# Hedgehog attention and Sinkhorn-routed experts on one core: q projections on row halves, one exponential for a pair's scalings, the routing table in PSUM, and a new step order

## The chip, the core and the metric

One core of a Trainium2 chip runs the whole program in one launch. TensorE (PE in the profile, PEld for its weight loads), VectorE (DVE), ScalarE (ACT) and GpSimd (POOL) each work through a queue of their own, in the order in which the kernel was written out; SyncE (SP), POOL and ACT issue DMAs. The metric is the device time of one execution in microseconds, the median of several.

## The reference, cut to what matters

```python
def phi(x):                                   # x: q or k, [8 batches, 8 heads, 576, 64]
    proj = np.einsum('bhsd,df->bhsf', x, w_phi)             # 128 features
    proj = proj - np.max(np.abs(proj), axis=-1, keepdims=True)
    return np.concatenate([np.exp(proj), np.exp(-proj)], axis=-1)
kv = np.einsum('bhsf,bhsd->bhfd', k_p, v);  z = np.sum(k_p, axis=2)
x = np.einsum('bhsf,bhfd->bhsd', q_p, kv) / den             # den from q_p and z
# x as [4608, 512]; then 8 experts, all of them for every row
P = np.exp(x @ w_gate - max)                                # [4608, 8]
for _ in range(8):
    P /= P.sum(1, keepdims=True) + 1e-09
    P /= P.sum(0, keepdims=True) + 1e-09;  P *= N / E
for e in range(8):
    out += P[:, e:e + 1] * (np.maximum(x @ w1[e], 0.0) @ w2[e])
```

## The kernel before, in words

A planner (`Plan`) holds every instruction as an operation with an engine, a duration and the buffers that it reads and writes. It lists them out engine by engine: the one that can start first by its own model goes next, and among equals the one that was written first. `Links` is its model of two DMA lines (SP's and POOL's), `LINK` the table of rates, `Clock` its model of TensorE's clock. What comes out is a fixed order for each engine; on the chip an engine waits at the head of its queue for whatever is late.

**Attention.** 32 pairs of heads (8 batches of 4) go through steps that a string, `order`, names letter by letter: `l`, `e` load q, k, v; `t` turns q and k by a DMA transpose (batches 2 to 7; batches 0 and 1 are turned on TensorE); `a` projects k, takes the maxima of its absolute values (`maxes`, L614) and writes exp of plus and minus the projection (`exp`, L618); `q` projects q with tokens on partitions for its maxima; `p` projects q again with features on partitions for its exponentials; `b` multiplies keys and values; `n` and `m` form the numerators of the two heads (L905, L913, L918, L919); `c` turns the result into `xT`; `r` does the 64 remaining tokens of a batch; `g` the gate. `u` and `d` are expert 0 (first and second product, 24 and 20 steps), put between the others so that TensorE has work. A q or k projection of a pair holds two heads in 128 rows of contraction, 64 rows each, and `wphi2` is block-diagonal: half of each such product is by zeros.

The maxima lie in a small tile `m`. For a pair ACT takes two small exponentials: `em` of plus and minus k's maxima, which scales v (POOL, L810, then L816 for the column of ones), and `r` of minus twice q's maxima, which scales the first half of the numerators on DVE (L913). The rest step has the same two, `em_r` and `r_r`.

**Routing.** When attention's buffers are given up (`swap`), eight rounds run on DVE (L1161 to L1188): scale the table's columns, sum its rows, reciprocal, scale the rows, sum the columns, split the sums into three bf16 parts, add them over partitions by a product with ones (TensorE, `colw`), reciprocal. The tables lie in SBUF. TensorE meanwhile goes on with expert 0 (`up0`, `down0`), and the routing's eight products stand in its queue between these. P is ready after L1189.

**Experts 1 to 7.** Each product is done by a Strassen-like scheme (L1481, L1472, L1613); sums of quarters of x and of the weights are taken by `sub` (L1240) on DVE first. For expert 1 these sums also wait for P. `UNITS` holds orders of the steps, the first nine for expert 1.

PSUM has 8 banks; `PP`, `P1`, `PO` are rings of single banks.

Of the kernel before, what the change touches and what calls it, by code (L numbers as in the profile page):

```python
# [126 lines left out]
class Links:  # L127
# [13 lines left out]
    def step(self, t, work):  # L141
# [5 lines left out]
        if len(on) == 2:  # L147
            a, b = (x[0][2] for x in self.line)
            all_ = (0.61 if a.turn else 0.84) / (a.unit + b.unit)
            share = [all_ * a.unit, all_ * b.unit]  # L150
# [48 lines left out]
class Plan:  # L199
# [10 lines left out]
    def op(self, eng, dur, lat, fn, r=(), w=(), takes=(), nbytes=0, shared=False):  # L210
# [5 lines left out]
        o.shared, o.turn, o.unit, o.tiled = shared, False, 0, 0  # L216
# [54 lines left out]
    def schedule(self):  # L271
# [22 lines left out]
        while len(done) < len(self.ops) or links.next():  # L294
# [10 lines left out]
            if landed and (best is None or landed[0] <= best[0]):  # L305
                o = links.land(*landed)
                o.end = landed[0] + 1.0
                finish(o)
                continue
# [40 lines left out]
def kernel(  # L350
# [38 lines left out]
    colw = const.tile([128, 128], BF16, name="colw")  # L389
# [13 lines left out]
    wphi2f = wphi2.rearrange("p a b -> p (a b)")  # L403

# [17 lines left out]
    def pool(el, fn, r=(), w=()):  # L422
        plan.op("POOL", el * 1.68e-3 + 0.13, 0.15, fn, r, w, shared=True)

    LINK = {320: (325, 56), 150: (160, 40), 230: (470, 108), 250: (305, 50), 280: (380, 60),
            270: (500, 48), 90: (340, 75), 148: (265, 30), 160: (540, 50)}

    def dma(queue, nbytes, rate, fn, r=(), w=()):

        speed, unit = LINK.get(rate, (rate, 40))  # L430
        if nbytes == 2 << 20:
            speed, unit = 400, 150
        o = plan.op(queue, 0.8 if queue == "POOL" else 0.6, 0.0, fn, r, w, (), nbytes / speed)
        o.turn, o.unit = rate == 148, unit

    TI, GR, KM, QM, PM, NM, RM = 0, 0, 0, 0, 0, 0, 0
# [36 lines left out]
    ring(a_s, [128, NP], FP32, "r_r", 2)  # L473
    ring(a_s, [128, 3, 8], FP32, "m", 2, 1)
    ring(a_s, [128, 2, 8], FP32, "em", 2, 1)
    ring(a_s, [128, 2, NP], FP32, "em_r", 2)
    ring(a_t, [128, 2, 8, D1], BF16, "v", 2, 1)
    ring(a_s, [128, 2, 5], FP32, "r", 2, 1)
    ring(a_s, [128, 1, 5], FP32, "rec", 3, 1)
# [16 lines left out]
    ring("s_p", [128, NT], FP32, "rr", 1)  # L496
    ring("s_p", [128, 3, E], FP32, "cs", 1)
    ring("s_p", [128, E], FP32, "c_bc", 1)
# [125 lines left out]
    def two(merged):  # L624

        if merged:
            b = new("P2")
            return [b], [lambda: b()[:, 0:512], lambda: b()[:, 512:1024]]
        b = [new("PP") for _ in range(2)]
        return b, b  # L630

    def tokens(pp, stat, n, r, takes=()):

        if not TI:
            for c in range(n):
                pe(256, lambda c=c: mm(pp[1][2 * c // n]()[:, 1024 // n * c % 512:][:, 0:256],
                                       stat(c), wphi2f, True, True),
                   r + ["wphi2"], [pp[0][2 * c // n * (len(pp[0]) - 1)]], takes)
            return

        def rows():
            for c in range(n):
                for x in range(2):
                    nc.tensor.matmul(pp[1][x]()[:, 128 * c:128 * c + 128],
                                     lhsT=stat(c)[64 * x:64 * x + 64],
                                     rhs=wphi[64 * x:64 * x + 64], start=True, stop=True)

        o = plan.op("PE", n * 0.056, 0.22, rows, r + ["wphi"], pp[0], takes)
        o.tiled = 1

    def feature_rows(pt, mov, r):

        if not TI and not GR:
            for x in range(2):
                pe(512, lambda x=x: mm(pt[1][x]()[:, 0:512], wphi2[:, x, :], mov(), True, True),
                   r + ["wphi2"], [pt[0][x * (len(pt[0]) - 1)]])
            return

        def rows():
            for x in range(2):  # L660
                half = slice(64 * x, 64 * x + 64)
                nc.tensor.matmul(pt[1][x]()[:, 0:512], lhsT=wphi[half], rhs=mov()[half],
                                 start=True, stop=True)

        o = plan.op("PE", 0.222, 0.22, rows, r + ["wphi"], pt[0])
        o.tiled = 1

    def rest_a(b, t):
# [23 lines left out]
        r["r"] = new("r_r")  # L692
        r["em"] = new("em_r")
        own = r["E"] + r["T"] + [m, r["r"], r["em"]]
        pp = two(RM)
        tokens(pp, lambda c: rT()[:, c, :], NP, [rT], own)
        if TI:
            mk = [(m, x) for x in range(2)]
            for x in range(2):
                maxes(512, lambda x=x: m()[:, 2 * x], lambda x=x: pp[1][x]().rearrange(  # L700
                    "p (c f) -> p c f", c=NP), [pp[0][x * (1 - RM)]], [(m, x)])
            for x, s in ((0, 1.0), (1, -1.0)):
                exp(512, lambda x=x: r["E"][x]().rearrange("p a b -> p (a b)"),
                    lambda: pp[1][1](), s, pp[0][-1:], [(r["E"][x], 0)])
        else:
            mk = [(m, c) for c in range(2 - RM)]
            for c in range(2 - RM):
                n = NP // 2 * (1 + RM)

                def sc(c=c, n=n):  # L710
                    return pp[0][c]().rearrange("p (a b c) -> p a b c", a=n, b=2)

                maxes(256 * n, lambda c=c, n=n: m()[:, 0:3:2, n * c:n * c + n].rearrange(
                    "p b a -> p a b"), sc, [pp[0][c]], [(m, c)])
                for x, s in ((0, 1.0), (1, -1.0)):
                    exp(128 * n, lambda x=x, c=c, n=n: r["E"][x]()[:, n * c:n * c + n],
                        lambda sc=sc: sc()[:, :, 1, :], s, [pp[0][c]], [(r["E"][x], c)])
        r["Ek"] = [[(r["E"][x], c) for c in range(1 if TI else 2 - RM)] for x in range(2)]
# [7 lines left out]
        exp(10, lambda: r["r"](), lambda: m()[:, 0], -2.0, mk, [r["r"]])  # L726
        pool(8, lambda: nc.gpsimd.tensor_scalar_mul(m()[:, 1], m()[:, 2], -1.0), mk, [(m, "neg")])
        em, vd = r["em"], vrd[b % 2]
        exp(10, lambda: em(), lambda: m()[:, 1:3], 1.0, mk + [(m, "neg")], [em])
        for h in range(2):  # L730
# [4 lines left out]
                in1=em()[rows, :, :, None].to_broadcast([64, 2, NP, D]), op=ALU.mult),  # L735
                [(t["v"], h), em], [("vrd", b % 2, h)])
            pool(80, lambda rows=rows, h=h: nc.gpsimd.tensor_copy(
                out=vd[rows, :, :, h, D], in_=em()[rows]),
# [3 lines left out]
    def pair_a(b, pr, t):  # L742

        h0 = (2 * pr) % 4
        s = {}
        if b < 2:
# [26 lines left out]
        s["r"] = new("r")  # L773
        em = new("em")
        own = s["E"] + s["T"] + [s["v"], em, m, s["r"]]
        at = (0, 2)

        def scores(x, pp):

            merged = (QM, KM)[x]  # L780
            for i, buf in enumerate(pp[0]):
                n = 1 + merged
                if TI or (GR and x == 0):
                    def src(buf=buf, n=n):
                        return buf().rearrange("p (h c f) -> p h c f", h=n, c=4)

                    def part(full, i=i, n=n):
                        return full.rearrange("p (c h) f -> p h c f" if len(full.shape) == 3
                                              else "p (c h) -> p h c", h=2)[:, i:i + n]
                else:  # L790
                    def src(buf=buf, n=n):
# [1273 lines left out]
```

## Time and profile before

| | |
|---|---|
| time, median of 3 runs | 1009.07 us (1008.1 to 1009.47) |
| span of the profiled execution | 1007.1 us, some 2.0 us below the median |
| attention, by the last copy into `xT` | from 0 to about 203.8 us |
| routing, L1164's first start to L1189's end | 205.1 to 242.1 us |
| first product of expert 1 (L1481) | 244.2 us |
| busy: PE, DVE, ACT, POOL | 99%, 89%, 81%, 44% |

A matmul's record runs from its issue to its modelled end; the next one starts while it drains. What a matmul takes from TensorE is thus the distance between starts in a row of them, not its duration. The same holds for back-to-back instructions on ACT and DVE, whose records overlap.

### The profile page before, as it was taken

The numbers are of one execution on the slowest core, as the hardware profiler recorded it, in microseconds if no ns is written. First come the engines' busy times: TensorE is split into PE (matmuls) and PEld (weight loads), VectorE is DVE, ScalarE is ACT, GpSimd is POOL, SyncE is SP. The second block draws the span as 40 slices with busy tenths as digits, with TensorE's granted clock in tenths as the row PEclk, the third lists the DMA queues.
The fourth block names the chain that finished last, engine by engine and source line by source line (L and its number), as shares of the span: only waits on it lengthen the run. The fifth ranks groups of instructions, "written<-read, shape, count | busy, mean of one in ns | idle before, by whom it ended". The sixth has DMA issues, their size and how long they took to land.

```text
span 1007.1 us, 23304 instructions
## 1 busy us (share of the span) xinstructions
PE 993.4 (99%) x8376; PEld 728.2 (72%) x8376; DVE 897.1 (89%) x1999; ACT 813.2 (81%) x1930; POOL 447.0 (44%) x514
## 2 busy tenths in 40 slices
PE   7899999999999999999999999999999999999998
PEld 5666666644566877777777877787778777787775
DVE  7999998987898898899989898989889988989886
ACT  7999999835979788878878788778887888778884
POOL 5778674400133344434444444444443444344443
PEclk9999999999999999999999999999999999999999
DMA  9999999181136423282327133632246222724653
GB/s 253 190 194 171 166 152 145 38 170 56 53 119 148 145 97 98 84 186 96 112 97 166 46 100 127 135 127 99 97 119 176 97 98 84 148 79 143 206 177 126
DMA packets 129748, 128.86 MB, mean 128 GB/s; under 512 B 55776, under 2 KB 98272, under 8 KB 129632
## 3 DMA queue, kind: packets, MB, share of 16 engines
q1 hardware_dynamic: 97680, 103.33, 35.5%
q0 software_dynamic: 31648, 23.86, 17.4%
q8 instruction: 65, 1.06, 0.4%
q14 instruction: 51, 0.42, 0.1%
q10 hardware_dynamic: 304, 0.20, 0.1%
HBM read 122.50 MB, written 19.53 MB: 141 GB/s over the span
## 4 chain that ended last, share of the span: by engine, by line
PE 92%; ACT 3%; DVE 2%; DMA 2%; issue 1%; POOL 0%; SPq 0%; DVEq 0%
PE ps L1472 42%; PE ps L1481 21%; PE ps L622 15%; PE ps L1613 11%; PE ps L905 2%; DMA xp<-xT 1%; ACT k L618 1%; ACT q L618 1%; DMA xi<-X 1%; PE ps L752 0%; DVE m L614 0%; ACT wx L618 0%; DVE wx L614 0%; DMA acc<-in_k_dram 0%; PE ps L934 0%
## 5 line engine op out<-in xcount | busy, mean ns | idle before, releaser
L1881 POOL TENSOR_TENSOR acc<-acc,hx 128x512 f32<-128x512 f32 x186 | 235.1, 1271 | 403.4 <-ACT hx L1878 138.5
L1472 PEld LDWEIGHTS <-hs 128*128 128x128 bf16 x1984 | 194.1, 98 | 46.6 <-issue 0.2
L1878 ACT ACTIVATE hx<-ps,P 128x256 f32<-128x256 f32 x372 | 159.3, 484 | 53.3 <-PE ps L1472 51.9
L1866 DVE SCALAR_TENSOR_TENSOR acc<-ps,P,acc 128x256 f32<-128x256 f32 x372 | 162.0, 477 | 29.8 <-PE ps L1472 28.1
L1481 PE MATMUL ps<-xT,T 128*128 128x512 bf16 x608 | 170.7, 379 | 0.0
L1472 PEld LDWEIGHTS <-hx 128*128 128x128 bf16 x1488 | 145.6, 98 | 25.1
L1472 PE MATMUL ps<-hx,hs 128*128 128x256 bf16 x992 | 144.3, 273 | 0.0
L1682 DVE CUSTOM_DVE_ANT_0 hs<-ps,U 128x512 bf16<-128x512 f32 x192 | 124.7, 684 | 10.9 <-PE ps L1481 6.6
L1613 PE MATMUL ps<-xT 128*128 128x256 bf16 x576 | 125.4, 272 | 0.0
L1481 PEld LDWEIGHTS <-T 128*128 128x128 bf16 x672 | 65.7, 98 | 40.4
L1688 ACT ACTIVATE hs<-ps 128x512 bf16<-128x512 f32 x96 | 55.8, 598 | 41.1 <-PE ps L1481 39.7
L1472 PE MATMUL ps<-wx,hs 128*128 128x256 bf16 x560 | 78.5, 273 | 0.0
L622 PE MATMUL ps<-w,hx 128*128 128x512 bf16 x288 | 73.0, 379 | 0.0
L622 PE MATMUL ps<-xT,w 128*128 128x512 bf16 x288 | 72.9, 379 | 0.0
L1472 PE MATMUL ps<-wx,hx 128*128 128x256 bf16 x496 | 72.6, 273 | 0.0
L1682 DVE CUSTOM_DVE_ANT_0 hs<-ps,X 128x512 bf16<-128x512 f32 x96 | 65.1, 683 | 7.4 <-PE ps L1613 6.6
L1472 PE MATMUL ps<-hx 128*128 128x256 bf16 x496 | 71.2, 273 | 0.0
L1613 PEld LDWEIGHTS <-xT 128*128 128x128 bf16 x576 | 56.3, 98 | 17.4
L614 DVE TENSOR_REDUCE m<-ps 128x4 f32<-128x512 f32 x88 | 58.8, 680 | 4.2 <-PE ps L622 2.0
L1472 PE MATMUL ps<-w,hx 128*128 128x256 bf16 x432 | 62.2, 273 | 0.0
L1678 ACT COPY X<-ps 128x512 f32<-128x512 f32 x96 | 58.6, 611 | 2.5 <-DVE ps L1656 2.4
L1472 PE MATMUL ps<-w,hs 128*128 128x256 bf16 x432 | 60.2, 273 | 0.0
(174 smaller groups left out, 2256.4 us busy)
## 6 DMA issues: line engine op xcount, KB each, us to landing
xT<-xi SPq DMA_DIRECT2D x48, 448.0 KB, 4.3
xT<-xd SPq DMA_DIRECT2D x72, 256.0 KB, 3.9
wx<-in_moe_w_dram POOLq DMA_DIRECT2D x8, 1024.0 KB, 11.0
v_m<-in_v_dram SPq DMA_DIRECT2D x15, 512.0 KB, 5.0
out_dram<-acc SPq DMA_DIRECT2D x14, 512.0 KB, 2.9
w<-in_moe_w_dram POOLq DMA_DIRECT2D x6, 1024.0 KB, 11.0
xT<-xp SPq DMA_DIRECT2D x24, 256.0 KB, 2.7
qk<-in_k_dram POOLq DMA_DIRECT2D x12, 256.0 KB, 5.2
```

Source lines behind the costliest of these rows:

```text
L614: dve(el, lambda: nc.vector.tensor_reduce(out=dst(), in_=src(), axis=AX.X, op=ALU.max, apply_absolute_value=True), r, w)
L618: act(el, lambda: nc.scalar.activation(out=dst(), in_=src(), func=ACT.Exp, bias=0.0, scale=scale), r, w)
L622: nc.tensor.matmul(out_, lhsT=lhsT, rhs=rhs, start=start, stop=stop)
L1472: pe(256, lambda i=i, k=k, z=z: nc.tensor.matmul(bank()[:, 256 * i:256 * i + 256], lhsT=lhs(k, i), rhs=rhs(k), start=first and z, stop=k = ...
L1481: pe(512, lambda k=k: nc.tensor.matmul(bank().rearrange("p (a b) -> p a b", a=2), lhsT=lhs(k), rhs=rhs(k), start=first and k == 0, stop=k ...
L1613: pe(256, lambda: nc.tensor.matmul(halves_of(bank[q], n)(), lhsT=lhs(), rhs=t()[:, rhs, :], start=start, stop=True, skip_group_check=True) ...
L1678: act(512, lambda: nc.scalar.copy(out=flat(to[q])(), in_=bank[q]()), [bank[q]], [(to[q], 0), (to[q], 1)])
L1682: dve(515, lambda: nc.vector._custom_dve(ADD_SAT, out=out_(q, i, j), in0=bank[q]().rearrange("p (a b) -> p a b", a=2), in1=to[q](), s0=3.0 ...
L1688: act(512, lambda: nc.scalar.activation(out=out_(q, i, j), in_=bank[q]().rearrange("p (a b) -> p a b", a=2), func=ACT.Relu, bias=0.0, scal ...
L1866: dve(320, lambda n=n, ts=ts: nc.vector.scalar_tensor_tensor(out=acc[g][:, ts, 256 * j:256 * j + 256], in0=bank()[:, 256 * n:256 * n + 256 ...
L1878: act(370, lambda n=n: nc.scalar.activation(out=u()[:, n, :], in_=bank()[:, 256 * n:256 * n + 256], func=ACT.Copy, bias=0.0, scale=P[:, 4 ...
L1881: pool(695, lambda: nc.gpsimd.tensor_tensor(out=acc[g][:, 2 * i:2 * i + 2, 256 * j:256 * j + 256], in0=acc[g][:, 2 * i:2 * i + 2, 256 * j: ...
```

## The change

Six parts. (1) **q on row halves**, for pairs 8 to 31: steps `q` and `p` become one block of ten matmuls that contract over 64 rows each, one head's rows against `wphi` (the plain weights, twice, one copy on each half of the partitions), alternately on the upper and lower half; it takes four PSUM banks at once. (2) **One exponential a pair**: POOL multiplies the maxima of k and q by -1 and -2 (`signs`), and one ACT instruction writes all 24 values into `em`; the scaling of v moves from step `a` to behind step `q`. The rest step likewise. (3) **Routing in PSUM**: one bank holds the table, the row sums and the column sums; POOL writes a transposed copy of L, so that both sums run over neighbouring words; the ones product is fp32 and replaces the split into three parts. (4) For expert 1 the sums of w1 and of the first pair of x run on POOL instead of DVE, and those of w1 no longer wait for P. (5) `down0` of groups 5 and 6 is read by ACT alone. (6) The planner's DMA constants, `order` and the first nine entries of `UNITS` are new. (A switch `JOINT` for joined numerators is added; its sets are empty.)

```diff
@@ class Links
-        self.line[n].append([at + (3.1 if n else 1.6), o.nbytes / 1e3, o])
+        lag = (2.4 if n else 2.1) if o.turn else 3.1 if n else 1.6
...
-    LINK = {320: (325, 56), 150: (160, 40), 230: (470, 108), 250: (305, 50), 280: (380, 60),
...
+    LINK = {320: (352, 245), 150: (355, 28), 230: (447, 41), 250: (305, 50), 280: (404, 58),
...
+    ROWS = range(8, 32)
+    JOINT = {"k": (), "q": (), "p": (), "n": ()}
@@ pair_a: behind k's exponentials
-        pool(8, lambda: nc.gpsimd.tensor_scalar_mul(m()[:, 1], m()[:, 2], -1.0), mk, [(m, "neg")])
-        exp(16, lambda: em(), lambda: m()[:, 1:3], 1.0, mk + [(m, "neg")], [em])
-        pool(1024, lambda: nc.gpsimd.tensor_tensor(
-            out=s["v"]()[:, :, :, 0:D],
...
@@ pair_a, maxima()
-            if GR:
-                pts[0] = two(PM)
+            if halves_:
+                pts[0] = two(pm)
+                more = [z for y in pts[0] for z in y]
 
                 def rows():
                     for c in range(4):
                         for x in range(2):
                             half = slice(64 * x, 64 * x + 64)
-                            nc.tensor.matmul(pq[1][x]()[:, 128 * c:128 * c + 128],
+                            nc.tensor.matmul(banks_[x]()[:, 128 * c:128 * c + 128],
                                              lhsT=qkT(0, c, 1)[half], rhs=wphi[half],
                                              start=True, stop=True)
                     for x in range(2):
                         half = slice(64 * x, 64 * x + 64)
-                        nc.tensor.matmul(pts[0][1][x]()[:, 0:512], lhsT=wphi[half],
+                        nc.tensor.matmul(more[x]()[:, 0:512], lhsT=wphi[half],
                                          rhs=qkT(0, 0, 4)[half], start=True, stop=True)
...
-            exp(10, lambda: s["r"]()[:, :, 0:4],
-                lambda: m()[:, 0].rearrange("p (a b) -> p a b", a=2), -2.0,
-                mq, [(s["r"], 0)])
+            pool(16, lambda: nc.gpsimd.tensor_tensor(
+                out=m()[:, 1:3], in0=m()[:, 0:3:2],
+                in1=signs[:, 0:2, None].to_broadcast([128, 2, 8]), op=ALU.mult),
+                mk + mq + ["signs"], [(m, "neg")])
+            exp(24, lambda: em()[:, 0:24], lambda: m().rearrange("p a b -> p (a b)"), 1.0,
+                mk + mq + [(m, "neg")], [(em, 0)])
+            pool(1024, lambda: nc.gpsimd.tensor_tensor(
+                out=s["v"]()[:, :, :, 0:D],
...
@@ down0
-            if ts % 2:
+            if ts % 2 or g in (5, 6):
@@ routing, one round
+            if it:
+                dve(366, lambda: nc.vector.tensor_tensor(
+                    out=table(), in0=L, in1=c()[:, None, :].to_broadcast([128, NT, E]),
+                    op=ALU.mult), lk, [bank])
+            dve(366, lambda src=table if it else lambda: L: nc.vector.tensor_reduce(
+                out=rr(), in_=src(), axis=AX.X, op=ALU.add), lk, [bank])
+            dve(291, lambda: nc.vector.reciprocal(out=rr(), in_=rr()), [], [bank])
+            dve(366, lambda: nc.vector.tensor_tensor(
+                out=turned(), in0=Lt(), in1=rr()[:, None, :].to_broadcast([128, E, NT]),
+                op=ALU.mult), [(side, 0)], [bank])
+            dve(366, lambda: nc.vector.tensor_reduce(
+                out=cs()[:, 0], in_=turned(), axis=AX.X, op=ALU.add), [bank], [cs])
+            pe(240, lambda: mm(sums(), ones(), cs()[:, 0], True, True), [cs, (side, 1)], [bank])
...
@@ sums_up
-        late = ["late"] + (["P"] if e == 1 else [])
+        late, eng = ["late"], pool if e == 1 else dve
```

How the orders move, at three places. First TensorE in attention: where steps `q` and `p` of a pair stand side by side before the change (`wphi_90` is `wphi2`, `qkT` the turned q):

```order
L622 LDWEIGHTS qkT
L622 MATMUL ps<-wphi_90,qkT 128x256
L622 LDWEIGHTS wphi_90
L622 MATMUL ps<-qkT,wphi_90 128x512
L622 LDWEIGHTS wphi_90
L622 MATMUL ps<-qkT,wphi_90 128x512
L905 LDWEIGHTS q_2093
L905 MATMUL ps<-kv,q_2093 128x65
```

These are the last of four 256-column products, then the two 512-column ones and the next step. And the end of such a block after the change, with the expert-0 product behind it:

```order
L804 LDWEIGHTS qkT
L804 MATMUL ps<-wphi,qkT 128x128
L809 LDWEIGHTS wphi
L809 MATMUL ps<-qkT,wphi 128x512
L809 LDWEIGHTS wphi
L809 MATMUL ps<-qkT,wphi 128x512
L623 LDWEIGHTS hx
L623 MATMUL ps<-w_1061,hx 128x512
```

Six products (four of 256 columns, two of 512) became ten (eight of 128, two of 512), in one piece. Second, DVE in the routing, one round before and one round after (L1161 and L1194 scale the columns, L1167 and L1200 the rows):

```order
L1185 TENSOR_REDUCE c_bc<-ps 128x8
L1188 RECIPROCAL c_bc<-c_bc 128x8
L1161 TENSOR_TENSOR T<-L,c_bc 128x288
L1164 TENSOR_REDUCE rr<-T 128x36
L1166 RECIPROCAL rr<-rr 128x36
L1167 TENSOR_TENSOR T<-L,rr 128x288
L1170 TENSOR_REDUCE cs<-T 128x8
L1179 TENSOR_TENSOR cs<-cs 128x8 x2
```

```order
L1194 TENSOR_TENSOR ps<-L,ps 128x288
L1197 TENSOR_REDUCE ps<-ps 128x36
L1199 RECIPROCAL ps<-ps 128x36
L1200 TENSOR_TENSOR ps<-T,ps 128x288
L1203 TENSOR_REDUCE cs<-ps 128x8
L1207 RECIPROCAL ps<-ps 128x8
```

Nine instructions a round became six. In TensorE's queue the eight routing products now stand exactly 14 expert-0 products of 512 columns apart, where before it was 18 to 24; 20 such products lie between the gate's last product and the first routing product, and 13 between the last routing product and the first product of expert 1. Third, POOL behind attention's last scaling of v (`X` holds sums of x, `T` and `wx` sums of w1):

```order
L824 TENSOR_TENSOR v<-v_m,em 128x16x64
L831 CAST v<-em 128x16
L518 DMA wx<-in_moe_w_dram 128x4x1024
L518 DMA wx<-in_moe_w_dram 128x8x512
L1261 TENSOR_TENSOR X<-xT 128x1024
L1189 COPY T<-L 128x288
L1261 TENSOR_TENSOR xT<-xT 128x2x2x256
L1261 TENSOR_TENSOR X<-xT 128x1024
L1261 TENSOR_TENSOR X<-xT 128x256
L1261 TENSOR_TENSOR X<-xT,X 128x1024
L1261 TENSOR_TENSOR T<-wx 128x1024
```

Before, the two weight loads were followed there by expert 1's additions to `acc`; the sums stood in DVE's queue. SP's queue is the same in its first 25 DMAs.

More of the change, by code (lines that the diff above doesn't have):

```diff
@@ L651, in feature_rows @@
[L651 to L666, printed above, removed]
+        return [b] if merged else [b[:1], b[1:]]
@@ L668, in rest_a, with feature_rows @@
+    def feature_rows(pp, mov, r):
+        for x in range(2):
+            pe(512, lambda x=x: mm(pp[x]()[:, 0:512], wphi2[:, x, :], mov(), True, True),
+               r + ["wphi2"], [pp[x]])
     def rest_a(b, t):
```

401 lines of the change are left out of this document (203 added, 198 removed), and 50 rows, old and new, of the table UNITS.

## The prediction

> **What bounds the kernel now.** First the page: span, busy time by engine, and the chain of work that ended last.
>
> ```profile
> span 1007.1 us, 23304 instructions
> PE 993.4 (99%) x8376; PEld 728.2 (72%) x8376; DVE 897.1 (89%) x1999; ACT 813.2 (81%) x1930; POOL 447.0 (44%) x514
> ...
> PE 92%; ACT 3%; DVE 2%; DMA 2%; issue 1%; POOL 0%; SPq 0%; DVEq 0%
> ```
>
> The chain is TensorE for 92%, so an edit counts by what it takes from TensorE's queue or by an idle gap that it opens or closes there. A 99% average hides stages, so next come the windows at the stage bounds (columns: length, then busy time and instructions of PE, PEld, DVE, ACT, POOL, then PE clock, DMA share, GB/s): attention's start, the rest of attention, routing, expert 1, all others.
>
> ```profile
> 0.00:60.00 60.00, 50.63 (x533) 35.40 (x534) 54.43 (x117) 54.70 (x136) 42.62 (x74) 1.00 1.12 223
> 60.00:204.00 144.00, 143.67 (x1715) 94.70 (x1714) 131.78 (x311) 135.55 (x330) 90.33 (x146) 1.00 0.94 136
> 204.00:244.00 40.00, 39.92 (x209) 18.14 (x206) 34.34 (x97) 15.95 (x29) 1.29 (x2) 1.00 0.53 114
> 244.00:352.00 108.00, 108.00 (x746) 72.83 (x745) 92.58 (x225) 91.86 (x185) 29.48 (x24) 1.00 0.41 119
> 352.00:1007.10 655.10, 651.23 (x5187) 507.14 (x5185) 583.96 (x1254) 515.10 (x1254) 283.28 (x270) 1.00 0.41 120
> ```
>
> TensorE is idle for 9.4 us in the first 60, for 0.3 in the next 144, 0.1 in routing, 0 in expert 1. From 60 us on it alone sets the pace, with ACT at 94% and DVE at 92% close behind until 204. After 352 nothing changes in the code. The first 60 us in slices of ten show another bound:
>
> ```profile
> 10.00:20.00 10.00, 7.90 (x54) 4.88 (x53) 9.95 (x17) 9.71 (x27) 8.55 (x13) 1.00 1.20 298
> ...
> 40.00:50.00 10.00, 9.53 (x120) 6.50 (x120) 9.93 (x24) 10.00 (x28) 8.07 (x17) 1.00 1.31 173
> 50.00:60.00 10.00, 9.63 (x119) 6.47 (x117) 10.00 (x25) 10.00 (x26) 9.86 (x14) 1.00 1.12 234
> ```
>
> There DVE and ACT are full and TensorE waits for them. So the start is bought with ACT and DVE time, the rest of attention with TensorE time.
>
> **The change part by part.** *q on row halves.* The time that a matmul takes is the distance of starts in TensorE's timeline:
>
> ```profile
> 191.98 0.59 PE L622 MATMUL ps<-qkT,wphi 128*128 128x512 bf16 x2
> 192.41 0.60 PE L622 MATMUL ps<-wphi,qkT 128*128 128x256 bf16 x4
> 192.84 0.19 PE L905 MATMUL ps<-wx 128*128 128x65 bf16 x1
> ...
> 197.55 0.39 PE L944 MATMUL ps<-ident,xb 128*128 128x128 bf16 x4
> 197.78 0.17 PE L622 MATMUL ps<-wgate,xT 128*128 128x8 bf16 x1
> ```
>
> Two of 512 columns take 0.43 us, four of 256 take 0.43, four of 128 take 0.23. A pair's q costs 0.43 + 0.43 = 0.86 now. No row shows 64-row products, so both ends: side by side, the block takes 4 x 0.0575 + 0.215 = 0.445, one after the other 8 x 0.0575 + 0.43 = 0.89. I take the first, since the two halves share neither rows nor banks. That is 24 x (0.445 - 0.86) = **-10.0 us**, all of it in the stretch where TensorE is the bound (other end +0.7).
>
> *Going into such a block and out again* is also in no row. At best nothing. At worst the array empties, so that the tail which the next product normally covers is seen: the two 512-column products last 0.59 for 0.43 of distance, a tail of 0.16; if a weight load (98 ns in the page's groups, below) can't be made ready either, 0.26. The block has two such edges, 48 in all: 0 to +12.5 us. I take 0.10 each, nearer to the bare tail than to the sum, as some of that tail is the results' way out: **+4.8**.
>
> The Trainium skill ("TensorEngine Tiling (Array Packing)", Key Properties) speaks against the change here: changing the tiling mode drains the engine. If a drain is the whole tail of 0.16 in the rows above, this term is +7.7 and the sum comes out 2.9 higher. No run so far shows such a change of mode.
>
> *Routing.* The rounds in DVE's timeline, and the products in TensorE's:
>
> ```profile
> 232.32 0.18 DVE L1185 TENSOR_REDUCE c_bc<-ps 128x8 f32<-128x24 f32 x1 [0.36 <-ACT hx L983]
> 232.54 0.20 DVE L1188 RECIPROCAL c_bc<-c_bc 128x8 f32<-128x8 f32 x1
> 232.78 0.46 DVE L1161 TENSOR_TENSOR T<-L,c_bc 128x288 f32<-128x288 f32 x1
> 233.27 0.45 DVE L1164 TENSOR_REDUCE rr<-T 128x36 f32<-128x288 f32 x1
> 233.76 0.38 DVE L1166 RECIPROCAL rr<-rr 128x36 f32<-128x36 f32 x1
> 234.17 0.46 DVE L1167 TENSOR_TENSOR T<-L,rr 128x288 f32<-128x288 f32 x1
> 234.67 0.68 DVE L1170 TENSOR_REDUCE cs<-T 128x8 f32<-128x288 f32 x1
> 235.38 0.37 DVE L1179 TENSOR_TENSOR cs<-cs 128x8 f32<-128x8 f32 x2
> 236.17 0.18 DVE L1185 TENSOR_REDUCE c_bc<-ps 128x8 f32<-128x24 f32 x1 [0.42 <-PE ps L622]
> ...
> 209.71 0.18 PE L622 MATMUL ps<-cs,colw 128*128 128x24 bf16 x1
> 209.74 1.45 PE L622 MATMUL ps<-w,hx 128*128 128x512 bf16 x6
> ...
> 244.18 1.67 PE L1481 MATMUL ps<-xT,wx 128*128 128x512 bf16 x7
> ```
>
> A quiet round lasts 236.17 - 232.32 = 3.85 us. After the change L1185 and the pair L1179 go, and the column sum runs over neighbours like L1164 (0.45 for 0.68): 0.20 + 0.46 + 0.45 + 0.38 + 0.46 + 0.45, six gaps of 0.035, and a wait for the product of 0.36 (bf16) to 0.69 (its longest in routing) make 2.97 to 3.30 a round. Eight rounds shrink from 37 us to 24 to 27. That itself is worth nothing: TensorE had 0.1 us of idle time in routing, covered by expert 0. What counts is that the routing products now stand 14 products apart, 14 x 0.216 = 3.02 us. In its queue TensorE stands still at each whose sum is late, with expert 0 behind it: (2.97 to 3.30) - 3.02 - the product's own time, seven times, so 0 to 2 us; I take **+0.5**, as the mid round is 3.13. The fp32 products themselves: now 0.03 each (209.71 to 209.74); the nearest fp32 row, L752 below, lasts 0.32. So 0 to +2.3, taken at 0.1 each, **+0.8**.
>
> *Sums on POOL.* POOL had two instructions in 204 to 244. Its nearest rows, and the weights that the sums wait for:
>
> ```profile
> L810 POOL TENSOR_TENSOR v<-v_m,em 128x1024 bf16<-128x1024 f32 x22 | 42.1, 1915 | 7.4 <-ACT em L618 7.2
> L1881 POOL TENSOR_TENSOR acc<-acc,hx 128x512 f32<-128x512 f32 x186 | 235.1, 1271 | 403.4 <-ACT hx L1878 138.5
> wx<-in_moe_w_dram POOLq DMA_DIRECT2D x2, 1024.0 KB, 13.5
> L752 PE MATMUL ps<-identf,acc 128*128 128x128 f32 x64 | 10.8, 317 | 4.4 <-DMA acc<-in_k_dram 3.8 <-ACT kr L618 0.3 <-DVE xb L919 0.2
> L1472 PEld LDWEIGHTS <-hs 128*128 128x128 bf16 x1984 | 194.1, 98 | 46.6 <-issue 0.2
> ```
>
> 1024 elements cost 1.9 (L810) to 2.5 us (twice L1881). Expert 1 needs eight of them, four of 256 (0.5 to 0.65) and the copy of L (0.6 to 0.75) first: 18 to 23.5 us in POOL's order, or, by the load, 13.5 + four large and three small = 23 to 25.5. Expert 1's first product stands behind 20 + 7 x 14 + 13 = 131 products, 28.3 us. So it is hidden, with 3 us to spare; if POOL were slower by half, TensorE would wait some 5 us there. **0**. The 5.5 us that DVE loses there (eight at 0.69) free no queue that TensorE waits on. The ACT copies of groups 5 and 6 lie where ACT is busy 16 us in 40: 0.
>
> *One exponential.* On ACT a small one costs the distance to the next start:
>
> ```profile
> 186.75 0.32 ACT L618 ACTIVATE r<-m 128x8 f32<-128x8 f32 x1
> 186.85 1.20 ACT L618 ACTIVATE wx<-ps 128x512 bf16<-128x512 f32 x2
> ...
> 190.19 0.40 ACT L618 ACTIVATE em<-m 128x16 f32<-128x16 f32 x1
> 190.29 2.25 ACT L618 ACTIVATE k<-ps 128x512 bf16<-128x512 f32 x4
> ```
>
> 0.10 us each; 40 of them go (32 pairs, 8 rests), 4 us of ACT. Only those in the first 60 us, some 11, touch the bound: -1.1 at best, **-0.5** because DVE is as full. In return v's scaling (1.9 us on POOL) waits for q's maxima. Behind the joint exponential in ACT's queue stand the exponentials of other pairs, and TensorE and DVE wait for these; the same wait for POOL exists now and its idle time is small, so I count **+0.5**, 0 to 3.
>
> *New order.* At most it wins the 9.4 us of idle time at the start; SP's loads there keep their order, and DVE and ACT stay full. **-1**, between -4 and +3.
>
> Sum: -10.0 + 4.8 + 0.5 + 0.8 - 0.5 + 0.5 - 1 = -4.9 us, from 1007.1 to 1002.2. The median stands 2.0 above this execution's span: **1004.1 us**.
>
> **The rivals.** *A: cheap edges.* If the edges cost 0.02 and the start gains 3, it is -10.0 + 1 + 0.5 + 0.8 - 0.5 + 0.5 - 3 = -10.7, 998.4. For it: the block is one piece. Against: ACT's 94%; but ACT could shrink from 144 us to 133 (135.55 less 28 small ones) before it is full.
>
> *B: ACT takes over.* If ACT keeps its 8.45 idle us of the middle stretch, attention shrinks by its 2.8 us of removed work alone, and with +1.3 from routing it ends at -1.5, 1007.6: no change. For it: ACT was 10.00 of 10 before. Against: its gaps there are mostly waits for TensorE.
>
> *C: slower, by banks.* The block takes four of eight PSUM banks at once, where q and its features took two and two. TensorE stands in front of it until the last is read, with expert 0 behind it in the queue:
>
> ```profile
> L618 ACT ACTIVATE q<-ps 128x512 bf16<-128x512 f32 x88 | 49.5, 687 | 0.2 <-PE ps L622 0.2
> ```
>
> If each block waits for one such reader more (0.69), that is +16.6, and the time 1004.1 + 16.6 = 1020.7; a wait of 0.20 a block already cancels the gain. Against: TensorE's idle time of 0.3 us in 144 says banks are rarely late now. The same side is reached if the halves run one after the other: +0.7 for -10.0, 1014.8.
>
> The Trainium skill ("TensorE: Matmul & The Clock Gate", Part 3, Measured speedup) gives 3.07 for four row tiles, less than their number. By the same share two would reach 1.54, and the block take 0.56, which adds 2.7 us to the sum. No row here bears on it.
>
> **How the numbers follow.** The forecast, 1001 to 1006.5: 0.45. A: 0.25. B: 0.15. C: 0.15. Those of A and B that lie between are in the range; from A's far end with a start of -4 (997.4) to the slow ends of edges (+7.7) and fp32 (+1.5) together, 1013; with half of C left out that keeps 8 in 10: 997 to 1012. About 2 us, 0.2%, is the least that a measurement can tell from no change. Faster by that: the forecast, A and a sliver of B: 0.72. Within it: 0.13. Slower: 0.15.
>
> **What would show it.** Right: L804's and L809's starts put a block at some 0.45 us; a 65- or 512-column product behind it starts about 0.1 late; expert 1's first product stands near 239 for 244.18; the fp32 products of routing lie 3.1 to 3.3 us apart. Wrong: blocks of 0.9 us, idle time of TensorE before them put down to ACT or DVE (C), or TensorE idle throughout attention with ACT full (B). Expert 2 on should keep its length.

## The result and the profile after

| | before | after |
|---|---|---|
| median of 4 runs each | 1008.67 us (1008.1 to 1009.47) | 1014.05 us (1013.78 to 1014.92) |
| ratio, with its 95% interval | | 1.0057 [1.0043, 1.0071] |
| span of the profiled execution | 1007.1 us | 1012.4 us |

Forecast were 1004.1 us and a range of 997 to 1012; the time rose by 5.4 us where it was to fall by 4.9, and lies outside the range. First the page of after: span, busy time by engine, the chain of waits.

```profile
span 1012.4 us, 23469 instructions
PE 989.4 (98%) x8480; PEld 719.1 (71%) x8480; DVE 884.9 (87%) x1951; ACT 811.7 (80%) x1894; POOL 469.9 (46%) x539
...
PE 89%; DVE 5%; DMA 3%; ACT 1%; issue 1%; POOL 1%; SPq 0%; DVEq 0%; POOLq 0%; ACTq 0%
```

TensorE is busy 4 us less than before and ends 5 us later; its share of the chain falls from 92% to 89%, VectorE's rises from 2% to 5%. The windows at the same bounds as before (columns as there):

```profile
0.00:60.00 60.00, 46.88 (x538) 33.08 (x539) 53.85 (x117) 52.34 (x119) 40.76 (x79) 1.00 1.00 208
60.00:204.00 144.00, 139.98 (x1769) 85.99 (x1768) 130.58 (x301) 133.71 (x307) 89.51 (x145) 1.00 0.96 142
204.00:244.00 40.00, 39.60 (x238) 19.61 (x237) 23.92 (x60) 19.37 (x35) 26.75 (x23) 1.00 0.53 114
244.00:352.00 108.00, 106.75 (x717) 69.80 (x716) 87.75 (x213) 88.32 (x175) 28.00 (x23) 1.00 0.41 118
```

In the 144 us of attention TensorE now stands idle for 4.0 us where it was 0.3, while ScalarE and VectorE still stand at 93% and 91%. The first 60 us, in which only one block of row halves stands, lose too: 13.1 us of idle time for 9.4, and TensorE's wait for VectorE's maxima there grows from 0.6 to 2.6 us (before, then after; columns: who waits for whom, us in total, times, longest):

```profile
PE ps L622 <- DVE m L614: 0.6, 2, 0.3
```

```profile
PE ps L623 <- DVE m L615: 2.6, 4, 1.7
```

Attention's end can be read from the last gate products in TensorE's timeline, of before and then of after:

```profile
203.51 0.94 PE L622 MATMUL ps<-wgate,xT 128*128 128x8 bf16 x32
```

```profile
207.33 0.94 PE L623 MATMUL ps<-wgate,xT 128*128 128x8 bf16 x32
```

That is +3.8 us in this pair of executions. But the new order also puts more of expert 0 ahead of this mark, as the groups of its products up to the mark show (before, then after):

```profile
L622 PE MATMUL ps<-xT,w 128*128 128x512 bf16 x208 | 54.4, 379 | 0.0
L622 PE MATMUL ps<-w,hx 128*128 128x512 bf16 x161 | 43.1, 379 | 0.0
```

```profile
L623 PE MATMUL ps<-xT,w 128*128 128x512 bf16 x220 | 59.3, 379 | 1.8 <-DMA xT<-wx 1.8
L623 PE MATMUL ps<-w,hx 128*128 128x512 bf16 x161 | 46.2, 379 | 0.4 <-DVE m L615 0.4
```

Twelve products of 0.216 us are 2.6 us of work done earlier, so that like for like, and by this pair alone, attention is only some 1.2 us longer, and what lies behind it some 4.1. The mark also scatters: executions with the very same attention gave 202.28 (e3) and 204.38 (e10) for that of before, 204.94 (e12) and 208.38 (e4) for that of after. Below, the timed runs decide, and a mark only between kernels of one order and where it moves by more than that.

The blocks of row halves themselves, in TensorE's timeline of after:

```profile
172.25 0.38 PE L623 MATMUL ps<-w,hx 128*128 128x512 bf16 x1
172.57 0.40 PE L804 MATMUL ps<-wphi,qkT 64*128 64x128 bf16 x8
172.80 0.38 PE L809 MATMUL ps<-qkT,wphi 64*128 64x512 bf16 x2
173.11 0.30 PE L887 MATMUL ps<-kv,q 128*128 128x65 bf16 x4
```

Eight products of 64 rows take 0.23 us, two of 512 columns 0.31 with the way out, and the way in adds 0.10 to the 0.216 of the product ahead (172.57 - 172.25 = 0.32). So q of a pair costs 0.10 + 0.54 = 0.64 us for 0.86: 24 x 0.22 = 5.3 us less, as forecast (5.2). The sum failed elsewhere. What TensorE waited for in attention:

```profile
PE ps L623 <- DMA xT<-wx: 1.8, 1, 1.8
PE ps L623 <- DMA qkT<-qk: 1.3, 1, 1.3
PE ps L623 <- DVE m L615: 0.4, 2, 0.2
PE ps L887 <- DVE ps L908: 0.2, 1, 0.2
```

Two late transposes stand out, 3.1 us, and the first theory was built on them.

### The profile page after: what moved, and what is told of

Read it like the earlier page. It is cut to its first block, busy times and chain, and to the rows that moved or that the text cites. A ratio compares the mean times of both kernels' runs of the same rounds, so it can differ in the third digit from the quotient of the medians.

```text
span 1012.4 us, 23469 instructions
## 1 busy us (share of the span) xinstructions
PE 989.4 (98%) x8480; PEld 719.1 (71%) x8480; DVE 884.9 (87%) x1951; ACT 811.7 (80%) x1894; POOL 469.9 (46%) x539
## 3 DMA queue, kind: packets, MB, share of 16 engines
q8 instruction: 66, 1.08, 0.4%
## 4 chain that ended last, share of the span: by engine, by line
PE 89%; DVE 5%; DMA 3%; ACT 1%; issue 1%; POOL 1%; SPq 0%; DVEq 0%; POOLq 0%; ACTq 0%
PE ps L1493 40%; PE ps L1502 20%; PE ps L623 15%; PE ps L1634 11%; PE ps L887 1%; DMA xT<-wx 1%; DVE m L615 1%; DMA qkT<-qk 1%; PE ps L804 1%; DVE hx L1261 1%; ACT wx L619 1%; DVE acc L1887 1%; PE ps L809 0%; POOL acc L1902 0%; DMA acc<-in_q_dram 0%
## 5 line engine op out<-in xcount | busy, mean ns | idle before, releaser
L623 PE MATMUL ps<-w,hx 128*128 128x512 bf16 x288 | 76.9, 379 | 0.4 <-DVE m L615 0.4
L623 PE MATMUL ps<-xT,w 128*128 128x512 bf16 x288 | 75.4, 379 | 1.8 <-DMA xT<-wx 1.8
## 6 DMA issues: line engine op xcount, KB each, us to landing
wx<-in_moe_w_dram POOLq DMA_DIRECT2D x8, 1024.0 KB, 10.3
```

Source lines behind the costliest of these rows:

```text
L623: nc.tensor.matmul(out_, lhsT=lhsT, rhs=rhs, start=start, stop=stop)
```

## The experiments

Two theories at the start. **W**: the row halves are worth their 5.3 us, and new waits, the two transposes ahead of all, take them back. **B**: ScalarE, VectorE and the PSUM banks that they free hold attention, so that shorter products only become waits (the prediction's rival B). A third, **S**, came with the runs: the planner's order fits only the set of durations for which it was found. Each run is compared with runs of before that were taken along with it. A difference in us is that of the two medians; the ratio is estimated from all runs, and differs from it by up to 0.8 us (e6).

| run | median, us | to before, us | ratio [95%] |
|---|---|---|---|
| after | 1014.05 | +5.4 | 1.0057 [1.0043, 1.0071] |
| e1 after, q as full products | 1015.14 | +6.7 | 1.0071 [1.0058, 1.0084] |
| e2 after, two waits moved | 1013.95 | +5.5 | 1.0056 [1.0042, 1.0070] |
| e3 attention of before, rest of after | 1012.09 | +3.7 | 1.0039 [1.0027, 1.0052] |
| e4 after, sums on VectorE | 1015.16 | +6.7 | 1.0067 [1.0054, 1.0079] |
| e5 after, ScalarE and VectorE lighter | 1010.68 | +2.1 | 1.0023 [1.0012, 1.0033] |
| e6 e5 with q as full products | 1014.20 | +5.6 | 1.0048 [1.0035, 1.0061] |
| e7 before, ScalarE and VectorE lighter | 1007.09 | -1.5 | 0.9986 [0.9978, 0.9995] |
| e8 after, VectorE lighter | 1011.75 | +3.2 | 1.0032 [1.0020, 1.0044] |
| e9 before, row halves alone | 1015.97 | +7.6 | 1.0078 [1.0063, 1.0093] |
| e10 before, new unit orders alone | 1010.86 | +2.5 | 1.0022 [1.0013, 1.0030] |
| e11 before, new transfer model alone | 1013.21 | +4.9 | 1.0047 [1.0034, 1.0060] |
| e12 after, routing of before | 1015.13 | +6.8 | 1.0071 [1.0056, 1.0085] |
| e13 before, TensorE lighter | 1008.96 | +0.6 | 1.0002 [0.9994, 1.0011] |
| e14 before, all three lighter | 1003.59 | -4.8 | 0.9957 [0.9940, 0.9974] |
| e15 after, new order with slack | 1012.87 | +4.5 | 1.0047 [1.0034, 1.0060] |
| e16 before, next to nothing changed | 1012.20 | +3.6 | 1.0042 [1.0028, 1.0056] |
| e17 e16 with one exponential | 1015.21 | +6.6 | 1.0067 [1.0055, 1.0079] |

**e1: what the row halves are worth in after.** The plan isn't touched, only the body of the block:

```diff
                 def rows():
                     for c in range(4):
-                        for x in range(2):
...
+                        nc.tensor.matmul(banks_[c // 2]()[:, 256 * (c % 2):256 * (c % 2) + 256],
+                                         lhsT=qkT(0, c, 1), rhs=wphi2f, start=True, stop=True)
                     for x in range(2):
-                        half = slice(64 * x, 64 * x + 64)
-                        nc.tensor.matmul(more[x]()[:, 0:512], lhsT=wphi[half],
+                        nc.tensor.matmul(more[x]()[:, 0:512], lhsT=wphi2[:, x, :],
...
```

> The kernel after with its plan untouched: the same order of every instruction on every engine, the same banks. Only the products inside the 24 blocks of q are those of before again (four 128x256 and two 128x512 instead of eight 64x128 and two 64x512). Theory W (the row halves gave what was forecast, and new waits of TensorE elsewhere took it back): 24 x (0.86 - 0.64) = 5.3 us more than after, about 1019.3. Rival B (in attention the banks, ScalarE and VectorE set the pace, so that shorter products only turn into waits): within 1.5 us of after, 1013 to 1015.5.

1.3 us more than after by the differences to before, with intervals that overlap; not 5.3. By the medians, three quarters of what the blocks save on TensorE don't reach the end. W falls in its first half.

**e2: the two late transposes.** After planning, the products that waited go behind those that stood after them; every other engine keeps its order:

```diff
+        MOVES = [(2154, 2148), (2588, 2998), (2589, 2998), (2590, 2998), (2591, 2998)]
...
-        done = self.schedule()
+        done = self.resequence(self.schedule())
```

> The kernel after, with the order on all engines but TensorE's kept and 62 of TensorE's 8256 instructions moved by a few places: the product that waited 1.75 us at 119.8 for a transposed xT comes after the 30 products that stood behind it, and the four k products that waited 1.26 us at 175.8 for a transposed qkT come after the 24 behind them. Theory W: both waits go and nothing else is late next, 2.4 to 3.0 us less than after, about 1011.3. Rival N (ScalarE and VectorE are behind by then, and the next wait takes their place): under 0.8 us less, 1013.3 or more.

The same time as after. Its waits of TensorE in attention, and from TensorE's timeline the row that took the place of the second one:

```profile
PE ps L930 <- DVE wx L923: 1.6, 1, 1.6
PE ps L666 <- DVE m L658: 0.4, 2, 0.2
```

```profile
177.50 0.28 PE L930 MATMUL ps<-wx 128*128 128x65 bf16 x4 [1.57 <-DVE wx L923]
```

Both DMA waits are gone, and at 177.5 the numerators wait 1.57 us for VectorE's copy of the key-value product instead. Moving the two longest waits of the list won nothing, since the next one takes their place: W falls in its second half too, as far as these two go.

**e3, e4, e10 and e12: what lies behind attention.** e3 is before with after's `routing`, `sums_up`, `sums_x`, `fine_x`, `down0` and first nine `UNITS`; e10 with these orders alone. e4 is after with the sums back on VectorE (those of w1 behind P, as before), e12 with the old routing:

```diff
 # e4, in sums_up (and sums_x, fine_x likewise)
-        late, eng = ["late"], pool if e == 1 else dve
+        late = ["late"] + (["P"] if e == 1 else [])
...
```

> The attention of before (its order, its transfer model, q as full products, two exponentials) with all of the change behind the attention: routing in PSUM, expert 1's first sums on GpSimd, the new orders of expert 1, ScalarE writing groups 5 and 6. By the two traces the attention ends 3.8 us later in after and the rest adds 1.5. Theory W: before + 1.5, about 1010.2 (1009.5 to 1011.2). Rival R (what is behind the attention loses most of it, by routing's stalls and late sums): 1012.5 or more.

> The kernel before with nothing changed but the nine new orders of expert 1's steps. e3 put 3.7 us on all that is behind the attention. If these orders carry it (they were found for sums and routing that end at other times): 1.5 to 3.5 us more than before, 1010 to 1012. If routing in PSUM or the sums on GpSimd carry it: within 0.7 us of before, 1007.9 to 1009.3.

> The kernel after with expert 1's first sums on VectorE again. Theory W (the sums on GpSimd are ready in time, hidden): within 0.8 us of after, 1013.3 to 1014.9. Rival P (the sums on GpSimd are late, and expert 1's orders were bought with them): 1 to 3 us less. Rival V (VectorE, which makes routing, can't take them in time): 1 to 3 us more.

> The kernel after with the routing of before (tables in SBUF, sums of three bf16 parts); attention, sums and expert 1's orders as in after. If routing in PSUM costs nothing at the end, as forecast (+1.3 at most with its fp32 products): 1012.5 to 1014.5. If it carries e3's loss: 1012 or less. If its earlier end was worth something: 1015 or more.

The part behind attention costs 3.7 us. The 1.5 expected came from the marks as they stand; with the 2.6 us of expert 0 that moved ahead of the mark they say 4.1, and e3 bears that out. The nine new orders cost 2.5 in before by themselves, though there they meet sums and routing for which they weren't made. Undoing the sums or the routing in after wins nothing (both medians are 1.3 to 1.4 higher, and the intervals overlap that of after), but neither run clears its part, since after's order doesn't fit what is put back and TensorE waits anew in routing (e12, then e4; after itself waits 0.4 there):

```profile
PE ps L626 <- DVE cs L1199: 3.3, 3, 1.7
```

```profile
PE ps L623 <- DVE cs L1203: 1.3, 1, 1.3
```

So e12's 1015.13, which falls under "its earlier end was worth something" in what was expected of it, doesn't show that; e4's 1.3 more, were it clear of noise, would be what its rival V expected. e3's other 1.2 us are about what the rows of routing add up to below (1.3); no run shows it.

**e5 to e8: take work from ScalarE and VectorE.** The plan stays as it is:

```diff
 # VectorE: maxima over half of the features
-            out=dst(), in_=src(), axis=AX.X, op=ALU.max, apply_absolute_value=True), r, w)
+            out=dst(), in_=src()[..., 0:32], axis=AX.X, op=ALU.max, apply_absolute_value=True), r, w)
 # ScalarE: exponentials of the query features over half of the columns (not in e8)
-                        "p a b c -> p a (b c)"), lambda bufs=bufs: over(bufs, 512), sg, bufs,
+                        "p a b c -> p a (b c)")[:, :, 0:256], lambda bufs=bufs: over(bufs, 512)[:, :, 0:256],
...
-                    lhsT=s["T"][x]()[:, j % 2, 2 * h + j // 2, :] if j < 4 else
+                    lhsT=s["T"][x]()[:, j % 2, j // 2, :] if j < 4 else
```

> The kernel after, its plan, its order and its banks unchanged, with shorter work on two engines in the attention: VectorE's maxima read 32 of the 64 features, ScalarE's exponentials of the query features cover half of the columns (and the second head uses the first one's). Left out: half of each maximum and the second head's query features. Theory B (ScalarE and VectorE, at 93% and 91% of the attention, and the banks they free set its pace; after e1 and e2 the likelier): TensorE's waits of the attention go, the last gate product comes 3 to 5 us earlier than in after, 1009 to 1011. Theory W (the waits come from transfers and from the order): within 1 us of after, 1013 to 1015.

> As e5, with q's blocks as full products (as in e1; the same left out as in e5). Theory B: with ScalarE and VectorE lighter TensorE sets the pace, and the blocks cost their full price, 4 to 5.3 us more than e5. Theory W: the row halves are worth about 1.3 us whatever the other engines do, as e1 less after: 0.8 to 2 us more than e5.

> The kernel before with the same lighter work on ScalarE and VectorE (the same left out as in e5). From 60 us on its TensorE waited 1.3 us in all, so by theory B it stands at TensorE's pace there and gains only in its first 60 us: 0.5 to 3 us less than before, 1005.5 to 1008. If it gains 4 us or more, ScalarE and VectorE paced the attention of before as well.

> As e5 with the maxima alone made shorter (VectorE), ScalarE as in after. Left out: half of each maximum. If VectorE is the one that is late, most of e5's gain, 2 us or more; if ScalarE is, under 1 us; if both together, about half of e5's.

Attention's windows in e5, and the last gate products of e5 and e6:

```profile
60.00:204.00 144.00, 139.06 (x1783) 87.30 (x1811) 96.58 (x305) 118.32 (x307) 88.83 (x144) 1.00 0.95 141
```

```profile
203.29 0.94 PE L623 MATMUL ps<-wgate,xT 128*128 128x8 bf16 x32
```

```profile
208.47 0.94 PE L623 MATMUL ps<-wgate,xT 128*128 128x8 bf16 x32
```

VectorE falls from 130.6 to 96.6 us, ScalarE from 133.7 to 118.3, and after gains 3.3 us, 2.2 of it by VectorE alone (e8, whose interval overlaps those of e5 and after, so that the split isn't firm). The row halves are now worth 3.5 us by the medians and 2.5 by the ratios (the intervals of e5 and e6, up to 1.0033 and from 1.0035, don't overlap), where they were worth 1.3 and 1.4. That points to theory B, but it is short of the 4 expected, and the step from 1.3 to 3.5 isn't clear of noise. The gate shows 5.2 (208.47 - 203.29), of which 1.7 come from one late transpose in the first 60 us (e5, then e6):

```profile
PE ps L623 <- DMA rT<-qk_r: 2.4, 1, 2.4
```

```profile
PE ps L623 <- DMA rT<-qk_r: 4.1, 1, 4.1
```

e7 gains 1.5 us in before, within the 0.5 to 3 expected.

**e9: the row halves alone in before.** `ROWS` and the block of ten products are put into before; the string and all tables are before's.

> The kernel before with the row halves alone: q's and the query features' products of pairs 8 to 31 as one block of 64-row products in four banks, everything else (order string, transfer model, two exponentials, routing, expert 1) as before; the planner deals its order anew from the same string. If TensorE sets the pace of before's attention, as the forecast read it: 24 x 0.22 = 5.3 us less, about 1003.3. Theory B (ScalarE and VectorE are as full as TensorE, and four banks are asked for at once): nothing or a loss, 1008 to 1013.

7.6 us slower, with 5.3 us less for TensorE to do: more than theory B expected (1013 at most). The run has three candidates: B, a wait for four banks at once, and an order dealt anew. Its trace speaks against the second. The products ahead of a block and the block, in TensorE's timeline of e9:

```profile
144.58 1.25 PE L624 MATMUL ps<-w,hx 128*128 128x512 bf16 x5
145.75 0.40 PE L833 MATMUL ps<-wphi,qkT 64*128 64x128 bf16 x8
```

Five products take 1.08 us, so this block starts 0.09 late, which is the way in alone. So do the other 23 of e9 (0.09 to 0.10 each), and 23 of the 24 in after (one comes 0.16 late): no block stands waiting for its banks. The other two candidates this run can't tell apart.

**e13 and e14: take work from TensorE alone, in before's own order.** Nothing is dealt anew and no bank is asked for earlier:

```diff
-                feature_rows(pt, lambda: qkT(0, 0, 4), [(t["T"], 0, h0 // 2)])
+                feature_rows(pt, lambda: qkT(0, 0, 4), [(t["T"], 0, h0 // 2)],
+                             256 if NP * b + pr >= 8 else 512)
...
 # e13 only: ScalarE reads the 256 columns twice
+                        lambda buf=buf: buf()[:, None, 0:256].to_broadcast([128, 2, 256])
```

> The kernel before, its plan and order unchanged, with less work for TensorE alone: the two products of the query features of pairs 8 to 31 cover 256 of 512 columns, 24 x 2 x (0.216 - 0.109) = 5.1 us of TensorE; ScalarE reads those columns twice, so its work stays. Left out: half of the query features of these pairs. If TensorE sets the pace of before's attention (as the forecast had it): 4 to 5 us less than before, about 1004. Theory B (VectorE, ScalarE and the banks are as full): 2 us less at most, 1006.5 to 1008.5.

> The kernel before with e7's lighter ScalarE and VectorE and e13's lighter TensorE together (left out: what e7 and e13 leave out). Theory B: only now is TensorE's time worth its price: 1.5 (e7) + 3 to 5 us less than before, 1002 to 1004.5. If TensorE's relief is worth as much as in e13, the three engines don't limit each other.

Attention in e13, and the last gate products of e13, e7 and e14:

```profile
60.00:204.00 144.00, 142.14 (x1707) 95.84 (x1732) 132.70 (x313) 135.76 (x332) 91.46 (x147) 1.00 0.89 136
```

```profile
202.06 0.94 PE L622 MATMUL ps<-wgate,xT 128*128 128x8 bf16 x32
```

```profile
202.75 0.95 PE L622 MATMUL ps<-wgate,xT 128*128 128x8 bf16 x32
```

```profile
197.61 0.94 PE L622 MATMUL ps<-wgate,xT 128*128 128x8 bf16 x32
```

This settles what TensorE's time was worth. 5.1 us less for TensorE move the time of before by nothing that can be measured (+0.02%, -0.06 to +0.11; the median is 0.6 up, and 0.5 above what even theory B expected). The same 5.1 us on top of e7's lighter engines move the gate by 5.1 (202.75 to 197.61) and the median by 3.5 (1007.09 to 1003.59; the intervals of e7 and e14 don't overlap). Lighter ScalarE and VectorE alone give 1.5, TensorE alone 0, the three together 4.8: in before TensorE and at least one of the other two stood at the limit at once. Transfers are the same in e13 and e14, so they can't be what held e13. Whether it is ScalarE, VectorE or the banks that they free isn't told apart.

**e11, e15 to e17: the order.** e11 is before with the planner's transfer model of after (`Links`, `LINK` and their constants) and nothing else. e16 is before rebuilt from after's code, where only the rests' merged exponential, three memsets, a copy of `w_phi` at the start, and one buffer for a pair's two exponentials are left of the change. e17 adds the one exponential of a pair. e15 is after with the transposes planned late, and the strings searched anew:

```diff
 # e15, in schedule()
-                o.end = landed[0] + (1.1 if o.turn else 1.0)
+                o.end = landed[0] + (2.6 if o.turn else 1.0)
...
```

> The kernel before with nothing changed but the planner's transfer model. Theory S (the order string was found under one model, and any change of the planned times deals the instructions anew, mostly worse): 2 to 4.5 us more than before, 1010.5 to 1013. Rival F (a model that fits the transfers better gives a plan that comes true): as before or less, 1008.7 at most.

> The kernel after with a step order and unit orders of expert 1 searched anew by the same planner, in which every DMA transpose lands 1.5 us later than its model has it, so that the order leaves slack for late ones. If the loss lies in an order that leaves the transposes no slack: 1009 to 1012. If late transposes aren't what costs (e2): 1013 or more.

> The kernel before, rebuilt from after's code: order string, transfer model, routing and expert 1 of before, q as full products, two exponentials for a pair; left from after are only the rests' one exponential in place of two, the three memsets of signs and GpSimd's copy of w_phi at the start. Theory S (any shift of the planned times deals the order anew, mostly worse): 1 to 4 us more than before, 1009.5 to 1012.5. If only costs count: as before, 1008 to 1009.

> As e16, with one exponential for a pair, and with it v's scaling behind q's maxima. If the merging costs an order that doesn't fit it: 2 to 4.5 us more than e16. If the new wait is hidden and ScalarE's 4 us count, as forecast: as e16 or up to 1 us less.

The transfer model, which changes no work at all, costs before 4.9 us, a little more than expected; e16's handful of small instructions costs 3.6. Both make the planner deal the instructions differently from the same string. So in these two runs a new deal had a price of some 4 us before anything was done, and e9's 7.6 and e17's 3.0 over e16 may hold such a price too. The change itself has a string of its own, so they don't measure how well that one fits. e15's order, another one for the same work, comes between its two expectations: it wins 1.2 us on after at best by the medians and 0.9 by the differences to before (the intervals overlap), and doesn't reach before. No version tried that computes the whole reference beats before.

## Why the prediction was wrong, point by point

**The step that failed**, and why nothing was won, is in the part on what bounds the kernel: "From 60 us on it alone sets the pace", and from it, that the row halves lie "in the stretch where TensorE is the bound". The rows quoted for it were right: 143.67 of 144 us busy, 0.3 idle. The reading was not. They say that TensorE had no slack; they don't say that ScalarE at 94% and VectorE at 92%, each with its own fixed order and with banks to hand back, had any that could be used. e13 is the direct measurement: 0 for 5.1 us. Rival B, with 0.15, was the mechanism, and its price of "no change" was nearly what e13 gave; but it named ScalarE, where e8 points to VectorE, if not firmly, and its 1007.6 is 6 us short of the measured time: that after comes out slower isn't B's.

The row halves are 3.9 us of the gap of 10.3 (5.4 slower for 4.9 faster). The other 6.4 lie in the new orders and what came with them, by the differences to before, each known to about 1.3 us and taken to add up:

| term | forecast | measured | from |
|---|---|---|---|
| row halves with their edges | -5.2 | -1.3 | e1 less after; -5.3 on TensorE by the block's rows |
| what lies behind attention | +1.3 | +3.7 | e3 |
| new order, one exponential, v's wait, in attention | -1.0 | +3.0 | after less e3, plus the 1.3 above |

*Block and edges* were right in size: 0.44 + 0.20 forecast, 0.64 measured. In part that is luck, since the 0.10 an edge was a choice between 0 and 0.26 for which no row spoke. Where the Trainium skill ("TensorEngine Tiling (Array Packing)", Key Properties) says that changing the mode drains the engine, the trace has a cost of 0.10 on each side; that fits, but is less than the whole tail of 0.16. The prediction's estimate of 0.56 for the block, from the figure that the Trainium skill has for four row tiles ("TensorE: Matmul & The Clock Gate", Part 3, Measured speedup), isn't borne out for two: eight half products take the 0.23 us of four whole ones.

*Routing* was right. A round in VectorE's timeline and the products in TensorE's:

```profile
226.03 0.22 DVE L1207 RECIPROCAL ps<-ps 128x8 f32<-128x8 f32 x1 [0.53 <-PE ps L623]
...
229.19 0.22 DVE L1207 RECIPROCAL ps<-ps 128x8 f32<-128x8 f32 x1 [0.53 <-PE ps L623]
```

```profile
213.00 0.36 PE L623 MATMUL ps<-cs,T 128*128 128x8 f32 x2 [0.40 <-DVE cs L1203]
216.24 0.28 PE L623 MATMUL ps<-cs,T 128*128 128x8 f32 x2
219.40 0.28 PE L623 MATMUL ps<-cs,T 128*128 128x8 f32 x2
...
238.13 1.46 PE L1502 MATMUL ps<-xT,wx 128*128 128x512 bf16 x6
```

3.16 us a round (2.97 to 3.30 forecast), products 3.16 apart for 3.02 of work between them, one stall of 0.40: 8 x 0.14 + 0.40, less the 8 x 0.03 of before, is 1.3 us, as forecast. Expert 1 starts at 238.13 (239 forecast), and no row of TensorE waits for GpSimd's sums. That start, 6 us earlier than before, is no gain: 131 products of expert 0 stand between the gate and it where it was 182, and the rest comes behind. What the sum lacked behind attention is the nine new orders: it gave them no term, and e10 measures 2.5, in before.

*The new order* was given -1, between -4 and +3. Together with the one exponential it is the second mis-sized term: +3.0 measured for -1.0, and the start, where it was to win, has 3.7 us more idle time. That a new deal can cost 3.6 to 4.9 us (e11, e16) makes the order the likelier part, but the cause of the 3.0 stays open: no run has the new order without the one exponential and v's wait, and e17's 3.0 over e16 holds the misfit of the old order too. Rival C, a wait in front of each block for four banks, isn't borne out by the 48 blocks of after and e9; what the four banks cost other steps no run shows. Expert 2 on keeps its length: from 362.49 in before and 367.70 in after TensorE has the same products in the same order, and both last 644.6 to 644.7 us to the end, so that the whole loss comes before that.

## What to carry to other kernels

An engine that is busy all the time is a bound only if the others have slack of their own: in a stage where three in-order queues stand at 99.8, 94 and 92%, price an edit by what it takes from all of them, or first take the time away in the unchanged order (e13) and see whether the end moves at all. Where a planner deals the order, an edit has to be compared with a new deal that changes next to nothing (here 3.6 to 4.9 us slower), and a version whose order was found for it with equal care would be needed to show the edit's own worth. A mark in a timeline compares two kernels only where the same work stands ahead of it. The longest waits of a trace need not be the ones that cost: move one and see what is late next.

## What the runs showed of the hardware

Two row halves run side by side: eight products of 64 x 128 take the 0.23 us of four of 128 x 128, and two of 64 x 512 take 0.31 us with the way out, where two of 128 x 512 take 0.43 (172.57 to 173.11 above). Going into such a block costs 0.10 us, and coming out about as much (0.31 less the 0.216 of one product). And small waits of TensorE don't show as idle time: in e13 its products are 5.1 us shorter and the gate moves by 1.45 at most (the mark scatters by as much), yet its busy time in attention falls by only 1.5 us (143.67 to 142.14). A 512-column record lasts 0.38 us for a turn of 0.216, so its modelled end covers a wait of up to 0.16; the view of waits lists none for TensorE there.
